# Gated stage of a fused fp32 kernel: order of the loads of x and the output's stores, half results from ScalarE's queue, order of the sums, and where the quarters of w3 · w_out are made

## The chip, the cores and the metric

The kernel runs on one core of one Trainium2 chip, as one launch. The time is the device time of the whole launch in microseconds (us).

## The reference

All tensors are float32. The kernel computes an attention with pooled keys and values, a mixture of four experts, and a gated layer, one after the other:

```python
k_p, v_p = k, v averaged over 8 neighbours          # batch 4, heads 8, seq 576, dim 64
attn = softmax(q @ k_p.T / 8) @ v_p                 # q: (4, 8, 576, 64)
x = attn, heads joined                              # (2304, 512)
p = domain_probs / sum(domain_probs)
x = sum over e of p[:, e] * (relu(x @ w1[e]) @ w2[e])    # 4 experts, 512 x 1024 and 1024 x 512
a = x @ w1                                          # moe2: (512, 1024)
b = x @ w2                                          # (512, 1024)
h = a * b @ w3                                      # a * b first; w3: (1024, 1024)
out = h @ w_out                                     # w_out: (1024, 512); out: (2304, 512)
```

## The kernel before

**Matmuls.** Each fp32 operand is split into a high part, rounded to the format that TensorE takes at full speed, and a low part, the difference. `hi_lo` does that: ScalarE copies the high part (L181), VectorE or GpSimd subtracts (L182). `mm3` (L176 to L178) makes one product of three matmuls: high by low, low by high, high by high. A 2 x 2 block product is done with seven block products instead of eight (Winograd's form of Strassen's method); the operands of these are the blocks A11, A12, A22 and the sums S1 to S4 of the left side, and B11, B21, B22 and T1 to T4 of the right side.

**The unit stage.** Since nothing stands between w3 and w_out, the kernel multiplies these two first: `w3_h` splits a piece of w3, and 24 units, run by `run_units` while the last expert ends (to 885.5 us), give the eight row blocks of w34 = w3 · w_out. `keep_w34` copies three (at last two) such blocks out of PSUM on ScalarE (L726) and stores them in DRAM (L727). Other work that belongs to the gated stage, the gate weights' sums and splits (`weights_of`, L797 to L800), stands between the units in a table `early`.

**The gated stage** (885.57 to 1270.5 us) goes over w34 in two halves, and in each half over the four batches of 576 tokens, in the order 2, 3, 0, 1. A batch has two parts. The first is four calls of `gated_rows(j)`; each makes a pair of row blocks of a and b with `seven` (products in the order p11, p22, p21, p12, and a `rest` of 18 matmuls, which `settle` runs inside the next call or inside the second part), multiplies them (L1390), sums and splits them into the right operand of the second part. The second part (84 matmuls) multiplies by a half of w34: p11 for the left column group, `settle`, p11 for the right one, p12, p22, p21, and then the sums (`add2`, L1501) by which the results are made out of the products. A batch has 252 matmuls in all.

In **half 0** the results are sums of half of the inner dimension: `give` copies them (L1481) and stores them in `half_d` through SyncE's queue (L1482), eight stores a batch. Beside it `prepare_x` makes the operand of x for the next batch (four subtractions L939 to L942, then splits), and `put_away` stores it in DRAM (`kept`) for half 1. In **half 1** `fetch_x` (L964) loads that operand back, in two pieces kc = 0 and kc = 1 of six transfers each; kc = 1 has about 2.0 MB. The halves are loaded (L1457); `give` adds (L1485), turns a tile of 128 x 288 on VectorE (L1487) into a buffer of `rawpool`, which has four such, and issues four stores of the output per tile (L1491), 32 a batch, all from SyncE's queue.

The pieces of w34 for a half (its A and S operands, `make_w34`, for n = 0 and 1) are made from rows loaded by `load_w34`, inside the first batch of each half, at j = 1 and 2. In the last batch of half 0 (called `swap` in the code) `weights_of` also makes the gate weights of half 1. PSUM banks come from a ring of eight; the first four products of a batch are written into the banks that p11[0], p11[1], p12[0] and p12[1] of the batch before had (the number in brackets is the column group g).

All instructions of an engine run in the order in which the code issues them. A transfer is issued by an engine's queue, also in order: where one has to wait, those behind it wait too.

## Time and profile before

| | before |
|---|---|
| median of 3 runs | 1274.4 us (1273.94 to 1275.97) |
| profiled execution | 1272.21 us, span of its profile 1270.5 us |
| busy: TensorE, VectorE, ScalarE, GpSimd | 1170.4 (92%), 767.1 (60%), 466.3 (37%), 514.8 us (41%) |
| mean granted clock of TensorE | 0.97 of full |

The span is the stretch that the profile covers; the execution's own time is 1.7 us longer. PE is TensorE's matmuls, PEld its weight loads, DVE VectorE, ACT ScalarE, POOL GpSimd, SP SyncE; SPq and ACTq are the queues in which SyncE and ScalarE issue transfers. PEclk is the clock granted to TensorE as a share of full speed. A time in square brackets is how long the engine stood idle before that instruction, with what ended the wait. Busy shares are means over the whole span, and the stages differ.

### The profile page before, as it was taken

The page shows a single profiled execution, that of the slowest core. Times are in us where ns is not written, and L with a number is a line of the kernel's source. Part 1 is how long each engine was busy: PE and PEld are TensorE (multiplying, and loading weights), DVE is VectorE, ACT ScalarE, POOL GpSimd, SP SyncE. Part 2 cuts the span into 40 slices and gives each one's busy share as a digit, 9 for nine tenths or more (in the row PEclk, how much of TensorE's full clock was granted, in tenths as well). Part 3 has the DMA queues.
Part 4 walks back from the last instruction along what each step waited for, and adds up shares of the span by engine and source line. Part 5 has one row for each costly group of instructions (what it writes and reads, how often), then busy time and mean ns, then how long its engine had stood idle before and what let it go on. Part 6 is the DMA issues. An engine that isn't in the chain of part 4 may idle for free.

```text
span 1270.5 us, 20381 instructions
## 1 busy us (share of the span) xinstructions
PE 1170.4 (92%) x7034; PEld 1065.5 (84%) x7034; DVE 767.1 (60%) x1615; ACT 466.3 (37%) x1029; POOL 514.8 (41%) x597
## 2 busy tenths in 40 slices
PE   8999999999999999999999999999799987595874
PEld 6888889998988988998998998888798887495774
DVE  6766534654666665666656677566666676544634
ACT  4543332453412542422552421545444444231221
POOL 6955113454525565525674534400512245220211
PEclk9999999999999999999999999999899998897978
DMA  8963623557767367658467868566554367345242
GB/s 212 225 157 78 209 94 137 203 185 241 252 212 221 108 213 218 216 151 263 121 191 218 237 152 242 141 167 178 202 205 160 138 206 241 83 123 143 77 126 38
DMA packets 278040, 221.81 MB, mean 175 GB/s; under 512 B 132528, under 2 KB 232880, under 8 KB 277936
## 3 DMA queue, kind: packets, MB, share of 16 engines
q1 hardware_dynamic: 277648, 219.98, 57.6%
q8 instruction: 55, 0.90, 0.3%
q10 hardware_dynamic: 288, 0.52, 0.1%
q14 instruction: 49, 0.40, 0.1%
HBM read 146.51 MB, written 73.92 MB: 174 GB/s over the span
## 4 chain that ended last, share of the span: by engine, by line
PE 75%; DVE 10%; DMA 5%; ACT 4%; issue 3%; SPq 2%; POOL 1%; DVEq 0%; ACTq 0%; POOLq 0%
PE g L177 13%; PE g L176 13%; PE g L178 13%; PE s L176 11%; PE s L178 10%; PE s L177 10%; PE sc L506 1%; PE x_ps L560 1%; DMA xo<-kept 1%; DVE plain L1381 1%; ACT round L181 1%; PE at_ps L545 1%; SPq L1491 1%; DVE plain L1390 1%; DVE x5l L1381 1%
## 5 line engine op out<-in xcount | busy, mean ns | idle before, releaser
L182 POOL TENSOR_TENSOR round<-plain,round 128x576 fp32r<-128x576 f32 (+1 forms) x130 | 178.5, 1376 | 403.9 <-ACT round L181 305.6
L176 PE MATMUL s<-xo,wh 128*128 128x288 f32 x840 | 255.2, 304 | 41.6 <-DMA xo<-kept 30.8
L178 PE MATMUL s<-xo,wh 128*128 128x288 f32 x840 | 252.3, 300 | 0.0
L177 PE MATMUL s<-xo,wl 128*128 128x288 f32 x840 | 251.5, 299 | 0.0
L176 PE MATMUL g<-w,round 128*128 128x512 f32 x540 | 211.7, 392 | 0.0
L177 PE MATMUL g<-w,round 128*128 128x512 f32 x540 | 211.2, 391 | 0.1
L178 PE MATMUL g<-w,round 128*128 128x512 f32 x540 | 210.9, 391 | 0.0
L176 PEld LDWEIGHTS s<-xo,wh 128*128 128x128 f32 x840 | 161.7, 193 | 47.4 <-DMA xo<-kept 32.6
L177 PEld LDWEIGHTS s<-xo,wl 128*128 128x128 f32 x840 | 162.1, 193 | 1.0
L178 PEld LDWEIGHTS s<-xo,wh 128*128 128x128 f32 x840 | 162.2, 193 | 0.0
L1004 ACT ACTIVATE plain<-s 128x288 f32<-128x288 f32 x80 | 32.7, 408 | 257.7 <-PE s L178 256.5
L1000 DVE TENSOR_TENSOR s<-s,plain 128x288 f32<-128x288 f32 x160 | 73.7, 461 | 78.3 <-PE s L178 75.2
L178 PEld LDWEIGHTS g<-w,round 128*128 128x128 f32 x540 | 101.3, 188 | 21.5
L176 PEld LDWEIGHTS g<-w,round 128*128 128x128 f32 x540 | 101.5, 188 | 20.1 <-issue 0.8
L177 PEld LDWEIGHTS g<-w,round 128*128 128x128 f32 x540 | 101.4, 188 | 19.6 <-DVE round L698 0.4
L181 ACT ACTIVATE round<-plain 128x576 fp32r<-128x576 f32 (+2 forms) x147 | 90.5, 626 | 45.7 <-DVE plain L1381 31.0
L294 POOL TENSOR_TENSOR x5l<-x5l 128x256 uint32<-128x256 uint32 x80 | 59.3, 741 | 117.3 <-DVE x5l L293 115.8
L1222 ACT ACTIVATE plain<-s 128x288 f32<-128x288 f32 x144 | 53.0, 403 | 95.0 <-PE s L178 88.7
L176 PE MATMUL s<-round,w 128*128 128x288 f32 x224 | 68.8, 307 | 19.5 <-DVE plain L1390 8.6
L1000 DVE TENSOR_TENSOR plain<-s,pb 128x288 f32<-128x288 f32 x72 | 32.9, 458 | 62.6 <-ACT pb L1010 34.6
L1000 DVE TENSOR_TENSOR plain<-s,plain 128x288 f32<-128x288 f32 x80 | 36.2, 453 | 53.1 <-PE s L178 46.4
L698 DVE SCALAR_TENSOR_TENSOR round<-g,round 128x384 fp32r<-128x384 f32 x48 | 26.6, 553 | 69.1 <-ACT round L697 68.8
(270 smaller groups left out, 2550.3 us busy)
## 6 DMA issues: line engine op xcount, KB each, us to landing
xo<-keptx SPq DMA_DIRECT2D x63, 576.0 KB
raw<-in_moe_w_dram SPq DMA_DIRECT2D x64, 256.0 KB
plain<-acc SPq DMA_DIRECT2D x40, 256.0 KB
keptx<-xo SPq DMA_DIRECT2D x16, 576.0 KB
x5h<-in_moe_w_dram SPq DMA_DIRECT2D x128, 64.0 KB
x5h<-in_moe_w_dram SPq DMA_DIRECT2D x32, 256.0 KB
kept<-xo SPq DMA_DIRECT2D x12, 576.0 KB
acc<-plain SPq DMA_DIRECT2D x26, 256.0 KB
```

Source lines behind the costliest of these rows:

```text
L176: nc.tensor.matmul(ps, lh, rl, start=first, stop=False, skip_group_check=onto)
L177: nc.tensor.matmul(ps, ll, rh, start=False, stop=False, skip_group_check=onto)
L178: nc.tensor.matmul(ps, lh, rh, start=False, stop=last, skip_group_check=onto)
L181: nc.scalar.activation(hi, src, AF.Copy)
L182: (lo_eng or nc.vector).tensor_tensor(lo, src, hi.bitcast(F32), op=ALU.subtract)
L294: nc.gpsimd.tensor_tensor(au, au, bu, op=ALU.add)
L506: nc.tensor.matmul(sc[off:off + n, (hp % 2) * W:(hp % 2 + 1) * W], qT[:, hp, off:off + n], kT_t[b][:, hp * W:(hp + 1) * W], start=True, st ...
L698: nc.vector.scalar_tensor_tensor(hl, ps, 0.0, hh.bitcast(F32), op0=ALU.max, op1=ALU.subtract)
L1000: nc.vector.tensor_tensor(to, one, two, op=ALU.add)
L1004: nc.scalar.activation(x, p11, AF.Copy)
L1222: nc.scalar.activation(c[:, a], c[:, a] if bank is None else bank, AF.Relu)
L1381: nc.vector.tensor_tensor(to, one, two, op=op)
```

## The change

It does five things, all in the gated stage and the unit stage.

1. **Loads of x.** In half 1, the fetch of kc = 1 is called right after `settle` in the second part, so its six transfers stand in SyncE's queue ahead of all 32 stores of the batch; before, they stood between the two groups of 16. In half 0 the same call makes the four subtractions of `prepare_x` at that place, the first splits come ahead of the results, and the loads of the batch after next are issued earlier (`load_x`).
2. **Half results.** In half 0, six of a batch's eight half stores are issued by ScalarE, behind the copy that makes them; two stay in SyncE's queue.
3. **The order of the sums.** Both products p11 now stand ahead of `settle`. VectorE makes the sums with p12 for both column groups, then those with v, and only then the results are given. In `gated_rows` for j >= 2 the second multiplication follows the first.
4. **Quarters of w34.** The pieces for half 0 are made between the units, in four steps each, at units 10, 11, 13, 14 and 18, 19, 21, 22, with both splits on ScalarE and VectorE. Three of the four rows that they need stay in SBUF; the row of block 1 is stored, and read back into the place that block 5 had. In half 1 the pieces stay at j = 1 and 2, with A11 and S1 split on VectorE instead of GpSimd.
5. **Turned tiles** go to a ring of five buffers (`turns`) instead of four.

The core of the diff:

```diff
         def keep_w34(b, pss):
             for o, ps in enumerate(pss):
-                t = kept_rows.tile([P, DM], F32)
-                nc.scalar.activation(t, ps, AF.Copy)
-                nc.sync.dma_start(w34_d[w3_blocks[b][0] + o], t)
...
+                fc = w3_blocks[b][0] + o
+                t = row_tile((0, 1, 2, 2, 1, 0, 3, 3)[fc])
+                nc.scalar.activation(flat2(t), ps, AF.Copy)
+                if fc in (0, 2, 3):
+                    w34_raw[fc] = t
+                else:
+                    nc.sync.dma_start(w34_d[fc], flat2(t))
+            if b == 1:
+                w34_raw[1] = row_tile(0)
+                nc.sync.dma_start(flat2(w34_raw[1]), w34_d[1])
...
+            def one():
+                left, right = w34_raw[n], w34_raw[n + 2]
+                w34_raw["s"] = s()
+                nc.vector.tensor_tensor(w34_raw["s"][:, 0], left[:, 1], right[:, 1], op=ALU.add)
+                nc.vector.tensor_tensor(w34_raw["s"][:, 1], w34_raw["s"][:, 0], left[:, 0], op=ALU.subtract)
+                split(A11, left[:, :1], nc.vector)
+
+            def two():
+                left = w34_raw[n]
+                nc.vector.tensor_tensor(left[:, 1], left[:, 0], left[:, 1], op=ALU.subtract)
+                split(S1, w34_raw["s"], nc.vector)
+
+            def three():
+                split(A12, w34_raw[n + 2], other)
+
+            def four():
+                left, right = w34_raw.pop(n), w34_raw.pop(n + 2)
+                nc.vector.tensor_tensor(left[:, 0], right[:, 0], w34_raw.pop("s")[:, 1], op=ALU.subtract)
+                split(S3, left[:, 1:], other)
+                split(S4, left[:, :1], other)
...
+        for n, at in enumerate((10, 18)):
+            for m in range(4):
+                early.setdefault(at + m + (m > 1), []).append(lambda n=n, m=m: w34_pieces(n, lambda: row_tile(1), nc.vector)[m]())
...
+        turns = row(x5[0], 0, HALF_ROW, 5)
...
-                        nc.sync.dma_start(half_d[b][:, m, a * HB:(a + 1) * HB], ob)
+                        (nc.sync if ps is None else nc.scalar).dma_start(half_d[b][:, m, a * HB:(a + 1) * HB], ob)
...
-                    tt = rawpool.tile([P, HB], F32, tag="raw", name="tt")
+                    tt = turns.tile([P, HB], F32)
...
-                p11 = [bank_s()]
-                second_part(p11[0], 0, A11, B11, two)
-                nc.scalar.activation(x[0], p11[0], AF.Copy)
+                p11 = []
+                for g in two:
+                    p11.append(bank_s())
+                    second_part(p11[g], g, A11, B11, two)
+                    nc.scalar.activation(x[g], p11[g], AF.Copy)
                 settle()
-                p11.append(bank_s())
-                second_part(p11[1], 1, A11, B11, two)
-                nc.scalar.activation(x[1], p11[1], AF.Copy)
+                ahead = half == 0 and n_b < B - 2
+                next_x(1, first, 0)
+                if ahead:
+                    load_x(g_order[n_b + 2], 0)
...
                 for g in two:
                     second_part(p11[g], g, A12, B21, [1])
-                    if half:
-                        add2(halves[:, g + 2, 1], halves[:, g + 2, 1], v[g])
-                        ob = halves[:, g + 2, 1]
-                    else:
-                        ob = place(g + 2, 1)
-                    add2(ob, p12[g], ob if half else v[g])
+                for g in two:
+                    add2(obs[g], p12[g], obs[g] if half else v[g])
                     add2(p12[g], p12[g], u[g])
+                next_x(1, first, 1)
+                if half:
+                    for g in two:
+                        add2(obs[g], obs[g], v[g])
+                for g in two:
                     give(g, 0, p11[g])
-                    give(g + 2, 1, None, ob)
-                next_x(1, first, 0)
+                    give(g + 2, 1, None, obs[g])
```

**SyncE's queue, end of half 1's first batch and start of its second.** Before (`out_dram` is the output, `half_...` the stored halves, `kept` the stored operand of x, and w_68, round and edge the places that it is loaded into):

```order
L1457 DMA plain<-half_8717 128x576 x4
L1491 DMA out_dram<-tt 32x9x32 x16
L964 DMA w_68<-kept 128x288
L964 DMA w_68<-kept 128x576
L964 DMA round<-kept 128x1152
L964 DMA edge<-kept 128x288
L964 DMA round<-kept 128x576
L964 DMA edge<-kept 128x1152
L1491 DMA out_dram<-tt 32x9x32 x16
```

And now:

```order
L1485 DMA plain<-half_8743 128x576 x4
L987 DMA w_68<-kept 128x288
L987 DMA w_68<-kept 128x576
L987 DMA round<-kept 128x1152
L987 DMA edge<-kept 128x288
L987 DMA round<-kept 128x576
L987 DMA edge<-kept 128x1152
L1519 DMA out_dram<-x5h 32x9x32 x32
```

The six transfers out of `kept` have moved ahead of the first 16 stores, and the two groups of 16 stand together.

**VectorE, second part of the last batch.** Before, from the fifth sum on (s_12059 and s_12060 are the banks of p12, s_12075 and s_12076 those of p21; plain holds the halves, tt the turned tiles):

```order
L1501 TENSOR_TENSOR plain<-plain,pb 128x288
L1501 TENSOR_TENSOR plain<-s_12059,plain 128x288
L1501 TENSOR_TENSOR s_12059<-s_12059,plain 128x288
L1485 TENSOR_TENSOR plain<-s_12009,plain 128x288
L1487 STREAM_TRANSPOSE tt<-plain 128x288 x2
L1501 TENSOR_TENSOR plain<-plain,pb 128x288
L1501 TENSOR_TENSOR plain<-s_12060,plain 128x288
L1501 TENSOR_TENSOR s_12060<-s_12060,pb 128x288
L1485 TENSOR_TENSOR plain<-s_12051,plain 128x288
L1487 STREAM_TRANSPOSE tt<-plain 128x288 x2
L1485 TENSOR_TENSOR plain<-s_12075,plain 128x288
L1487 STREAM_TRANSPOSE tt<-plain 128x288
```

And now, from the last of ten sums on (here s_12023 and s_12024 are the banks of p12, s_12039 and s_12040 those of p21, and x5h holds the turned tiles):

```order
L1529 TENSOR_TENSOR plain<-plain,pb 128x288 x2
L1513 TENSOR_TENSOR plain<-s_11973,plain 128x288
L1515 STREAM_TRANSPOSE x5h<-plain 128x288 x2
L1513 TENSOR_TENSOR plain<-s_11981,plain 128x288
L1515 STREAM_TRANSPOSE x5h<-plain 128x288 x2
L1513 TENSOR_TENSOR plain<-s_12039,plain 128x288
L1515 STREAM_TRANSPOSE x5h<-plain 128x288
L1513 TENSOR_TENSOR plain<-s_12040,plain 128x288
L1515 STREAM_TRANSPOSE x5h<-plain 128x288
L1513 TENSOR_TENSOR plain<-s_12023,plain 128x288
L1515 STREAM_TRANSPOSE x5h<-plain 128x288
L1513 TENSOR_TENSOR plain<-s_12024,plain 128x288
```

Eight additions stood ahead of the first transpose, and eleven do now; the additions that read p12's banks stand ahead of the seventh and of the eighth transpose, as before.

**VectorE, near the end of the unit stage.** Before (raw holds a piece of w3, edge and round its low halves; wl are low halves of gate weights):

```order
L182 TENSOR_TENSOR wl<-plain,wh 128x512
L182 TENSOR_TENSOR wl<-plain,wh 128x256
L182 TENSOR_TENSOR round<-raw,round 128x256
L182 TENSOR_TENSOR edge<-raw,edge 128x256
L182 TENSOR_TENSOR wl<-x5l,wh 128x768
L182 TENSOR_TENSOR round<-x5l,round 128x256
L182 TENSOR_TENSOR edge<-raw,edge 128x256
L182 TENSOR_TENSOR round<-raw,round 128x256
```

And now (plain holds the rows of w34, w_68 the pieces' low halves):

```order
L756 TENSOR_TENSOR plain<-plain 128x256
L757 TENSOR_TENSOR plain<-plain 128x256
L182 TENSOR_TENSOR w_68<-plain,w_68 128x256
L182 TENSOR_TENSOR round<-raw,round 128x256
L762 TENSOR_TENSOR plain<-plain 128x256
L182 TENSOR_TENSOR w_68<-plain,w_68 128x512
L182 TENSOR_TENSOR edge<-raw,edge 128x256
L182 TENSOR_TENSOR wl<-x5l,wh 128x768
L182 TENSOR_TENSOR round<-x5l,round 128x256
L182 TENSOR_TENSOR edge<-raw,edge 128x256
L182 TENSOR_TENSOR w_68<-plain,w_68 128x512
L182 TENSOR_TENSOR round<-raw,round 128x256
```

The second piece's steps stand among the low halves of the units; L756 is the first operation that reads the row of block 1.

## Rows read from the trace of the kernel before

**Rows 1.** The chain that ended last, by engine (page)

```profile
PE 75%; DVE 10%; DMA 5%; ACT 4%; issue 3%; SPq 2%; POOL 1%; DVEq 0%; ACTq 0%; POOLq 0%
```

**Rows 2.** Windows: stretch length, busy by engine (instructions), granted clock, DMA share, GB/s

```profile
885.57:932.07 46.50, 39.01 (x255) 37.91 (x254) 29.69 (x61) 19.93 (x48) 20.73 (x20) 0.89 0.46 162
...
932.07:1048.45 116.38, 104.74 (x755) 100.70 (x754) 78.70 (x168) 52.19 (x122) 32.01 (x32) 1.00 0.53 189
...
1048.45:1098.90 50.45, 38.31 (x255) 36.05 (x254) 33.78 (x71) 20.99 (x52) 27.48 (x26) 0.93 0.46 152
...
1098.90:1254.65 155.75, 112.93 (x759) 107.87 (x757) 72.88 (x176) 34.50 (x84) 28.19 (x30) 0.85 0.41 113
```

**Rows 3.** Windows, two stretches of half 1's last batch

```profile
1217.64:1220.52 2.88, 2.88 (x13) 2.88 (x13) 0.92 (x2) 0.16 (x1) 0.00 (x0) 0.50 0.40 66
...
1226.00:1238.03 12.03, 11.91 (x90) 11.67 (x88) 6.41 (x16) 3.82 (x10) 3.44 (x4) 1.00 0.12 44
```

**Rows 4.** Waits, batches 1 to 3 of half 1: total, times, longest

```profile
PE s L176 <- DMA xo<-kept: 24.8, 4, 11.9
...
PE s L176 <- DMA edge<-kept: 11.8, 2, 11.5
...
PE s L176 <- DVE s L1501: 3.4, 3, 1.1
```

**Rows 5.** Timeline of SyncE's queue: start, length, what, count

```profile
1200.29 7.80 SPq L1491 DMA_DIRECT2D out_dram<-tt  x16
...
1208.19 2.77 SPq L964 DMA_DIRECT2D xo<-kept  x6
...
1211.06 10.46 SPq L1491 DMA_DIRECT2D out_dram<-tt  x16
```

**Rows 6.** Timeline of TensorE: start, length, what [idle before]

```profile
1213.88 0.61 PE L176 MATMUL s<-xo,wh 128*128 128x288 f32 x1 [10.54 <-DMA xo<-kept]
...
1217.24 0.61 PE L176 MATMUL s<-xo,wh 128*128 128x288 f32 x1 [1.55 <-DMA xo<-kept]
```

**Rows 7.** Timeline of VectorE in the last batch

```profile
1248.10 0.46 DVE L1501 TENSOR_TENSOR plain<-s,plain 128x288 f32<-128x288 f32 x1 [2.26 <-PE s L178]
...
1251.65 0.84 DVE L1487 STREAM_TRANSPOSE tt<-plain 128x288 f32<-128x288 f32 x2
...
1257.41 0.48 DVE L1487 STREAM_TRANSPOSE tt<-plain 128x288 f32<-128x288 f32 x1 [1.27 <-DMA out_dram<-tt]
```

**Rows 8.** Timeline of SyncE's queue, last batch

```profile
1252.15 15.98 SPq L1491 DMA_DIRECT2D out_dram<-tt  x32
```

**Rows 9.** Timeline of TensorE, half 1, batch 0, 25th matmul

```profile
1061.05 0.29 PE L176 MATMUL s<-xo,wh 128*128 128x288 f32 x1
```

**Rows 10.** Timeline of ScalarE, from half 0 to half 1

```profile
1053.72 0.69 ACT L1481 ACTIVATE plain<-s 128x288 f32<-128x288 f32 x2
```

**Rows 11.** Waits, first batch of half 0

```profile
PE s L176 <- DVE plain L1390: 7.2, 3, 3.6
```

**Rows 12.** Timeline of VectorE, last units and first gated batch

```profile
876.78 0.42 DVE L799 TENSOR_TENSOR x5l<-plain 128x256 f32<-128x256 f32 x1
...
877.45 1.02 DVE L182 TENSOR_TENSOR wl<-plain,wh 128x512 fp32r<-128x512 f32 x2
...
892.93 0.46 DVE L939 TENSOR_TENSOR x5h<-plain 128x288 f32<-128x288 f32 x1 [2.98 <-DMA plain<-turned]
```

**Rows 13.** Timeline of TensorE, unit stage

```profile
872.55 0.50 PE L177 MATMUL g<-round,edge 128*128 128x512 f32 x1 [0.58 <-DVE edge L182]
```

**Rows 14.** Timeline of ScalarE, unit stage

```profile
873.32 1.99 ACT L726 ACTIVATE plain<-g 128x512 f32<-128x512 f32 x3 [0.71 <-PE g L178]
```

**Rows 15.** Timeline of TensorE, second part of a batch of half 0

```profile
954.74 0.37 PE L176 MATMUL s<-round,w 128*128 128x288 f32 x1 [0.48 <-DVE plain L1390]
...
963.35 0.40 PE L176 MATMUL s<-round,w 128*128 128x288 f32 x1 [0.38 <-ACT pb L1509]
```

**Rows 16.** Timeline of ScalarE's queue, first loads of the kernel

```profile
0.81 0.88 ACTq L405 DMA_DIRECT2D plain<-in_k_dram  x2
```

More of the change, by code (lines that the diff above doesn't have):

```diff
@@ L719, in fused_kernel, with row_tile, flat2 @@
         w34_t.update((n, tuple(Ring(w2_area, [(2 * n + m) * W34]).tile([P, 7, 2 * P], F32R) for m in range(2))) for n in range(2))
-        kept_rows = row(plain, 0, ROW, 3)
+        stage_rows = [Ring(plain, [ROW * n]) for n in range(4)]
         w34_raw = {}
+        def row_tile(n):
+            return stage_rows[n].tile([P, 2, 2 * P], F32)
+        def flat2(t):
+            return t.rearrange("p a m -> p (a m)")
         def keep_w34(b, pss):
             for o, ps in enumerate(pss):
-                t = kept_rows.tile([P, DM], F32)
-                nc.scalar.activation(t, ps, AF.Copy)
-                nc.sync.dma_start(w34_d[w3_blocks[b][0] + o], t)
@@ new lines, in keep_w34, with load_w34 @@
+                t = row_tile((0, 1, 2, 2, 1, 0, 3, 3)[fc])
[7 more added lines that the diff above has]
+                nc.sync.dma_start(flat2(w34_raw[1]), w34_d[1])
+        def load_w34(n):
+            for fc in (n, n + 2):
+                w34_raw[fc] = rawpool.tile([P, 2, 2 * P], F32, tag="raw", name="w34r")
+                nc.sync.dma_start(flat2(w34_raw[fc]), w34_d[NJ + fc])
@@ new lines, in w34_pieces, with split @@
+        def w34_pieces(n, s, other):
+            def split(a, src, eng):
+                m = src.shape[1]
+                hi_lo(*(flat2(t[:, a:a + m]) for t in w34_t[n]), flat2(src), eng)
+            def one():
[15 more added lines that the diff above has]
+                split(S4, left[:, :1], other)
+            return one, two, three, four
@@ L1402, in sink @@
                     mult(1)
+                    mult(0)
                     add(up[:, 1], g[:, 1], up[:, 1])
@@ L1406, in sink @@
                         split_g(n, T2, up[:, :1], VE)
-                    mult(0)
-                    if n:
                         split_g(n, T3, up[:, 1:], VE)
@@ L1443, in fused_kernel @@
                         weights_of(3)
-                    if n_b == 0 and j in (1, 2):
-                        make_w34(j - 1)
-                    if n_b == 0 and j < 2:
-                        load_w34(half, j)
+                    if half == 1 and n_b == 0 and j in (1, 2):
+                        for f in w34_pieces(j - 1, lambda: rawpool.tile([P, 2, 2 * P], F32, tag="raw", name="w34s"), nc.gpsimd):
+                            f()
+                    if half == 1 and n_b == 0 and j < 2:
+                        load_w34(j)
                     if half == 0 and n_b == 0 and j < 2:
@@ L1523, in fused_kernel @@
                     add2(u[g], p22[g], x[g])
+                obs = [place(g + 2, 1) for g in two]
                 for g in two:
@@ L1544, in fused_kernel @@
                     give(g + 2, 0, p21[g])
-                next_x(1, first, 1)
                 next_x(1, first, 2)
+                if ahead:
+                    load_x(g_order[n_b + 2], 1)
                 if swap:
@@ L1551, in fused_kernel @@
                     give(g, 1, p12[g])
-                if half == 0 and n_b < B - 2:
-                    for kc in range(2):
-                        load_x(g_order[n_b + 2], kc)
                 put_away()
```

19 lines of the change are left out of this document (removed).

## The prediction

> **What bounds the kernel now.** I read the chain that ended last first: three quarters of the span run over TensorE [rows 1], so a change pays only where TensorE stands still or runs slowly. Then I cut the gated stage into stretches that end where a batch's last matmul ends [rows 2]. A batch always has 252 matmuls. At the full granted clock one takes 12.03/90 = 0.1337 us, in a low stretch 2.88/12 = 0.24 us (12 of the 13 start in it) [rows 3], so a batch needs 252 x 0.1337 = 33.7 us. Half 0 (its last three batches: 116.38, or 38.8 each) is near that; half 1 is not: 155.75 for batches 1 to 3, or 51.9 each, at clock 0.85. The waits of that stretch [rows 4] say why: TensorE stood 24.8 + 11.8 = 36.6 us for transfers out of kept. In SyncE's queue [rows 5] those six transfers start only when the first 16 stores of the output have been issued (1200.29 to 1208.09), and TensorE, which ran dry at 1203.3, gets its two pieces at 1213.88 and 1217.24 [rows 6]; the second is 9.05 us after the first issue. Behind each such wait comes a stretch at clock 0.50.
>
> **1. The fetch ahead of the stores (half 1, batches 1 to 3).** The six transfers are now issued when the second part's first products are set going, 84 - 12 = 72 matmuls or 9.6 us before the boundary T (I write T for the end of a batch's last matmul). By the 5.7 to 9.05 us of [rows 5, 6] the data lie there between T - 4 and T - 0.5; they are needed at T + 0.4 at the earliest. So the waits for kept go, and the low clock with them.
>
> What is late next is VectorE. In the last batch [rows 7] the first sum starts at u0 = 1248.10, the first transpose at u0 + 3.55, and the first store [rows 8] at s0 = u0 + 4.05; 32 stores take 15.98, so 2.0 per tile. The sixth transpose waits 1.27 for a buffer and starts at s0 + 5.26: with four buffers the k-th starts at s0 + 2.0 (k - 4) + 1.25. After, eleven additions stand ahead of the first transpose instead of eight. Eight took 3.55, 0.44 each with their small waits; three more, back to back at some 0.3 to 0.4, make s0 = u0 + 5.0, less if the small waits go: I take u0 + 4.9. That is about T - 0.1, as TensorE has some 38 of the 84 matmuls left at u0 (5.0 us). With five buffers the sixth transpose starts at s0 + 3.25, the seventh at s0 + 5.25. The additions that read the last two banks (those of p12) stand behind these two on VectorE, and the next batch's third and fourth products write into these banks. The first is free at about T + 3.15 + 0.48 + 0.46 = T + 4.1, with the semaphore T + 4.15; TensorE wants it 12 matmuls after T, at T + 1.6: **2.55 us of wait**. The second is free at T + 6.15 and wanted at T + 4.95: **1.2 us more**. The 3.4 us in three waits for the sums [rows 4] go, since the sums now stand ahead of the transposes. New length of a batch: 33.7 + 3.75 = 37.45. Gain: 155.75 - 3 x 37.45 = **43.4 us**. Bounds: without any boundary wait 54.6; with twice it 32; if such a wait again drops the clock, as the wait of 10.54 did for some 20 matmuls (six of the first piece, and 3.3/0.24 = 14 from 1217.24 to 1220.52, [rows 3, 6]), 20 x 0.106 = 2.1 per batch less.
>
> **2. The last batch's end.** Nothing runs beside the last 32 stores. They start 0.85 later after u0 (4.9 instead of 4.05), while TensorE's 1.1 us stall before them goes; the span then ends s0 + 18.35 as now (1252.15 to 1270.50). Measured from the end of the batch, which part 1 counts, the stores begin at T - 0.1 instead of T - 2.5: **-2.4 us** (0 to -2.5).
>
> **3. Half 1, batch 0.** Before, its 25th matmul started at 1061.05 [rows 9], after the same two waits for kept and with its first matmuls at 0.24. After, the fetch precedes the gate loads and the half stores, and the third product waits for what now comes last: ScalarE's copies of the p12 banks at 1053.72 [rows 10], which stand behind the last of the new weights' splits; that work is not moved. First copy done 1054.1, 25th matmul at about 1054.6: **+6.4 us**. Bounds: 3, if the splits get later by the sums moved in front of them; 9, if they get earlier with the second part.
>
> **4. Quarters of w3 · w_out made between units.** The first gated batch loses its stalls for VectorE's L1390, which stood behind the pieces: 7.2 us in three [rows 11], and its low clock (0.89 of 46.50, [rows 2]). It should come near its neighbours' 38.8, with less to wait for at its start: 36 to 38, so +8.5 to +10.5; I take 10. The work goes into the unit stage. Of the two pieces' 18 VectorE operations, 14 are 128x256 at about 0.42 and 4 are 128x512 at 0.51 [rows 12]: 14 x 0.42 + 4 x 0.51 = 7.9 us. TensorE already waited there once for a low half (0.58, [rows 13]), and the low halves stand behind the pieces in VectorE's order; I charge 1.5 for that. The second piece needs the row that is read back: ScalarE's copies end at 875.3 [rows 14], the store has to be issued (0.5) and land (1.25, the buffer waits of [rows 7]), and the row has to come back, nearly 3 us as the reload that VectorE waited 2.98 for [rows 12]; so 880 to 881, where the unit's slot is at 877. The low half behind it is 4 late: 1.5 + 4 = 5.5. A clock that falls after such a wait costs 2.1 as above; I charge 1.5. Net 10 - 5.5 - 1.5 = **+3 us**. Bounds: -4 (all 7.9 on TensorE, 4 of wait, 2.1 of clock) and +7 (1.5 and 1.5 only).
>
> **5. Half 0's second part, three batches.** The product before settle takes away the two waits of 0.48 and 0.38 where TensorE stood for L1390 and for a copy [rows 15], with the slower first matmul behind each some +1.4 a batch. Against it, four subtractions (4 x 0.46 = 1.8) stand ahead of the sums, of which I let 0.75 reach TensorE, and six half stores are issued by ScalarE; an issue took 0.88/2 = 0.44 there [rows 16], so four of them put the next operand's last split off by 1.8, of which I let 1.05 through, as VectorE waits for ScalarE there only part of the time: 1.4 - 0.75 - 1.05 = -0.4 a batch. Over three batches **-1 us** (-4 to +3).
>
> The Trainium skill, "DMA: Bandwidth & Descriptors", section "Issuing engines are not separate DMA queues", says that transfers issued from several engines share the same 16 DMA engines and that only the issuing sequencer's time is saved, usually little. By it the move to ScalarE's queue saves SyncE about 6 issues a batch and nothing else. [Rows 16] agree as far as they go (a like issue time), and this is one reason why I give the move no gain; the sum is the same with or without the rule.
>
> **Sum.** 43.4 - 2.4 + 6.4 + 3 - 1 = 49.4. The profiled execution took 1272.2 (span 1270.5), so 1222.8; the median of the runs, 1274.4, is 2.2 higher, which gives **1225 us**.
>
> **Rivals.**
> A. The boundary wait doesn't come about, because VectorE runs through the reordered sums faster than I count: 49.4 + 3 x 3.75 = 60.7, so 1214; with part 4 at its best 1210. Against it: four stores per tile at 2.0 us are slower than VectorE's 0.94 per tile (0.46 + 0.48, [rows 7]), so some buffer must be waited for. Chance 0.12; range 1206 to 1214.
> B. Parts 3 to 5 go to their low bounds: the unit stage pays in full, ScalarE's issues stand in the splits' way. 43.4 - 2.4 + 3 - 4 - 4 = 36, with the clock falling at boundaries (3 x 2.1) 30: 1238 to 1244, and to 1255 if the boundary wait is twice as long too. For it: VectorE is nearly full in the unit stage. Chance 0.16.
> C. The fetch still comes late: it waits for its target's last reader, or its 2.0 MB and the halves' loads share the DMA engines. Then 36.6 us of wait shrink by no more than the 7.8 of the 16 stores: 3 x 8 = 24, less 2.4 and the rest at zero: 1250 to 1272. Against it: the target is the operand that this batch's rows have finished with by settle. Chance 0.06.
> D. Slower: TensorE's clock. A stretch at 0.50 costs 252 x (0.24 - 0.1337) = 26.8 us a batch. If the new, shorter but more frequent waits keep the granted clock low for more than 49.4/0.106 = 466 matmuls, not quite two batches, beyond today's, the gain is eaten, and it ends at 1277 or more. Against it: after a wait of 10.54 the clock stood at 0.50 until 1220.5 and at 1.00 from 1226 on [rows 3, 6]. Chance 0.04.
>
> **How the numbers follow.** The forecast, with 2 to 5 us left at each boundary, has 0.62 and its own range is 1214 to 1237. The 80% range reaches into A and B: 1208 to 1244. A, B, C and most of the forecast's tails are faster by more than 0.2% (2.5 us, about what a measurement tells from no change): 0.95; same 0.01; slower 0.04.
>
> **What would show it.** In the profile after: no wait of TensorE for kept in half 1 over 1 us; batches there of 36 to 39 us at clock 1.0; waits of TensorE for the additions of the last two banks, 2 to 3 and 1 us, and VectorE's transposes waiting for stores; a first gated batch of 36 to 38; the unit stage ending at about 891 instead of 885.6; the third product of half 1 waiting for ScalarE. I am wrong if batches 1 to 3 still hold waits for kept, or if the clock in half 1 stays under 0.95.

## The result and the profile after

| | before | changed |
|---|---|---|
| median | 1275.18 us (1273.94 to 1275.99, 4 runs) | 1235.78 us (1233.16 to 1236.57, 4 runs) |
| ratio | | 0.9688 (95% interval 0.9671 to 0.9706) |
| span of the profiled execution | 1270.5 us | 1231.4 us |

The changed kernel is 39.4 us faster; 49.4 had been forecast (to 1225 us), with a range of 1208 to 1244. The windows by stretch answer to [rows 2], this time cut where a batch's first matmul starts; the first is the first batch of half 0, then come three batches, the first batch of half 1, three batches, and the kernel's end:

```profile
895.42:934.09 38.67, 34.82 (x254) 33.71 (x252) 25.60 (x55) 15.75 (x38) 9.75 (x10) 1.00 0.51 180
934.09:1053.00 118.91, 105.68 (x759) 103.85 (x757) 78.91 (x167) 54.06 (x124) 34.25 (x33) 0.97 0.56 199
1053.00:1095.60 42.60, 36.44 (x255) 35.13 (x254) 31.96 (x72) 20.05 (x49) 22.21 (x22) 0.96 0.52 176
1095.60:1213.76 118.16, 109.92 (x758) 107.44 (x756) 71.00 (x175) 34.13 (x84) 28.93 (x30) 0.93 0.47 131
1213.76:1231.40 17.64, 0.16 (x2) 0.00 (x0) 4.43 (x11) 0.00 (x0) 0.00 (x0) 0.56 0.40 67
```

I took each batch's length from the start of its first matmul to that of the next batch's first:

| stretch | before | changed | difference |
|---|---|---|---|
| start of the gated stage | 885.57 | 895.42 | +9.85 |
| half 0, first batch | 46.23 | 38.67 | -7.56 |
| half 0, three more | 37.80 + 37.79 + 41.19 | 40.30 + 37.19 + 41.42 | +2.13 |
| half 1, first batch | 50.44 | 42.60 | -7.84 |
| half 1, three more | 50.67 + 53.09 + 51.87 | 39.56 + 38.94 + 39.66 | -37.47 |
| behind the last matmul | 15.85 | 17.64 | +1.79 |

The sum is -39.1, the difference of the spans. Of the 9.85 at the start, 1.8 were there before the units: the last 174 matmuls ahead of the gated stage begin at 846.83 instead of 845.07. They take 48.6 us instead of 40.5, so 8.1 arise in the unit stage. In four other runs with the same unit stage (below) they take 47.4 to 47.9, and the gated stage begins at 892.5 to 893.7.

In SyncE's queue of the changed kernel the fetch of kc = 1 now stands ahead of 32 stores in one row (the answer to [rows 5]; its last transfer is shown):

```profile
1087.48 0.43 SPq L987 DMA_DIRECT2D edge<-kept  x1
1095.23 16.96 SPq L1519 DMA_DIRECT2D out_dram<-x5h  x32
```

The last of six issues for kc = 1 is over at 1087.9, 7.7 us ahead of the boundary at 1095.60. No wait of TensorE for kept is left in half 1. What it waits for instead, in the timeline of TensorE at that boundary (the answer to [rows 6]):

```profile
1099.31 0.40 PE L176 MATMUL s<-xo,wh 128*128 128x288 f32 x1 [1.97 <-DVE plain L1513]
...
1101.22 0.61 PE L176 MATMUL s<-xo,wh 128*128 128x288 f32 x1 [0.65 <-DVE plain L1513]
1101.62 0.44 PE L177 MATMUL s<-xo,wl 128*128 128x288 f32 x1
1101.86 0.44 PE L178 MATMUL s<-xo,wh 128*128 128x288 f32 x1
```

The 13th matmul of the batch waits 1.97 and the 19th 0.65 for VectorE's L1513, the addition in `give`, and from there on the matmuls follow each other at 0.24 us, the step of the low clock. VectorE at the same place (the answer to [rows 7]):

```profile
1090.48 0.46 DVE L1529 TENSOR_TENSOR plain<-s,plain 128x288 f32<-128x288 f32 x1 [0.92 <-PE s L178]
...
1094.72 0.84 DVE L1515 STREAM_TRANSPOSE x5h<-plain 128x288 f32<-128x288 f32 x2
...
1098.43 0.48 DVE L1515 STREAM_TRANSPOSE x5h<-plain 128x288 f32<-128x288 f32 x1 [0.46 <-DMA out_dram<-x5h]
1098.83 0.42 DVE L1513 TENSOR_TENSOR plain<-s,plain 128x288 f32<-128x288 f32 x1
1100.34 0.48 DVE L1515 STREAM_TRANSPOSE x5h<-plain 128x288 f32<-128x288 f32 x1 [1.09 <-DMA out_dram<-x5h]
1100.74 0.42 DVE L1513 TENSOR_TENSOR plain<-s,plain 128x288 f32<-128x288 f32 x1
1102.41 0.48 DVE L1515 STREAM_TRANSPOSE x5h<-plain 128x288 f32<-128x288 f32 x1 [1.25 <-DMA out_dram<-x5h]
```

The sixth, seventh and eighth transposes wait 0.46, 1.09 and 1.25 for stores, and each of the additions at 1098.83 and 1100.74, which free the two banks, stands behind one of them. The sixth starts 3.20 behind the first store's issue, the seventh 5.11, the eighth 7.18; 3.25, 5.25 and 7.25 had been worked out.

### The profile page after: what moved, and what is told of

It is laid out like the page before. It is cut to its first block, busy times and chain, and to the rows that moved or that the text cites. A ratio compares the mean times of both kernels' runs of the same rounds, so it can differ in the third digit from the quotient of the medians.

```text
span 1231.4 us, 20352 instructions
## 1 busy us (share of the span) xinstructions
PE 1167.4 (95%) x7034; PEld 1065.5 (87%) x7034; DVE 767.7 (62%) x1629; ACT 466.6 (38%) x1029; POOL 502.0 (41%) x583
## 4 chain that ended last, share of the span: by engine, by line
PE 77%; DVE 8%; DMA 5%; SPq 3%; issue 3%; ACT 3%; POOL 1%; ACTq 0%; DVEq 0%; POOLq 0%
PE g L177 12%; PE g L178 12%; PE g L176 12%; PE s L176 12%; PE s L178 12%; PE s L177 12%; PE sc L506 1%; DMA x5h<-in_moe_w_out_dram 1%; PE x_ps L560 1%; PE at_ps L545 1%; SPq L1519 1%; DMA out_dram<-x5h 1%; SPq L475 1%; DVE plain L1529 1%; ACT round L181 1%
## 5 line engine op out<-in xcount | busy, mean ns | idle before, releaser
L182 POOL TENSOR_TENSOR round<-plain,round 128x576 fp32r<-128x576 f32 (+1 forms) x130 | 178.2, 1374 | 389.1 <-ACT round L181 175.7
L176 PEld LDWEIGHTS s<-xo,wh 128*128 128x128 f32 x840 | 159.9, 190 | 20.2 <-DVE plain L1513 6.7
L178 PEld LDWEIGHTS s<-xo,wh 128*128 128x128 f32 x840 | 160.0, 191 | 0.0
L1023 DVE TENSOR_TENSOR s<-s,plain 128x288 f32<-128x288 f32 x160 | 73.8, 461 | 73.9 <-PE s L178 70.1
L181 ACT ACTIVATE round<-plain 128x576 fp32r<-128x576 f32 (+2 forms) x147 | 90.5, 626 | 47.4 <-DVE plain L1408 33.8
L176 PE MATMUL s<-round,w 128*128 128x288 f32 x224 | 68.2, 305 | 10.6 <-ACT pb L1559 9.4
L1023 DVE TENSOR_TENSOR plain<-s,pb 128x288 f32<-128x288 f32 x72 | 33.0, 458 | 61.8 <-ACT pb L1033 35.5
L178 PE MATMUL s<-round,w 128*128 128x288 f32 x224 | 67.4, 301 | 0.0
```

Source lines behind the costliest of these rows:

```text
L176: nc.tensor.matmul(ps, lh, rl, start=first, stop=False, skip_group_check=onto)
L178: nc.tensor.matmul(ps, lh, rh, start=False, stop=last, skip_group_check=onto)
L181: nc.scalar.activation(hi, src, AF.Copy)
L182: (lo_eng or nc.vector).tensor_tensor(lo, src, hi.bitcast(F32), op=ALU.subtract)
L1023: nc.vector.tensor_tensor(to, one, two, op=ALU.add)
```

## The experiments

Each time stands beside that of the kernel before on the same chip (medians 1274.3 in the first two groups of runs, 1277.0 in the last).

### Eight places for the turned tiles

```diff
-                    tt = turns.tile([P, HB], F32)
+                    k = turned_n[0] % 8
+                    turned_n[0] += 1
+                    tt = turns.tile([P, HB], F32) if k < 5 else rawpool.tile([P, HB], F32, tag="raw", name="tt")
```

> The changed kernel, with the turned tiles of half 1 in eight places instead of five (the last three of a batch in the pool of raw tiles), so that no transpose waits for stores within a batch; order and stores are the same. Theory (the 2.0 and 1.0 us that TensorE waits at the three boundaries of half 1 come from the transposes' waits, and the stretch at 0.24 us a matmul behind them comes from these waits): both go, batches 1 to 3 fall from 118.2 us together to 102 to 104, and the kernel takes 1219 to 1223 where the changed one takes 1235.8. Rival 1 (the low clock there has a cause of its own): the waits go and the slow matmuls stay, 1226 to 1228. Rival 2 (the banks are late because VectorE itself is late): no change, 1234 to 1237.

Measured: 1220.24 us, ratio 0.9575 (0.9555 to 0.9595). Windows of half 1's batches 1 to 3, first of the changed kernel:

```profile
1095.60:1135.16 39.56, 36.94 (x254) 36.09 (x253) 23.65 (x59) 11.37 (x28) 9.69 (x10) 0.91 0.57 165
1135.16:1174.10 38.94, 35.95 (x255) 35.23 (x254) 23.68 (x59) 11.38 (x28) 9.70 (x10) 0.96 0.57 168
1174.10:1213.76 39.66, 37.04 (x254) 36.12 (x252) 23.67 (x59) 11.38 (x28) 9.54 (x10) 0.91 0.27 61
```

and of the kernel with eight places:

```profile
1092.90:1128.46 35.56, 34.02 (x254) 33.49 (x253) 23.66 (x59) 11.37 (x28) 9.69 (x10) 1.00 0.63 183
1128.46:1164.23 35.77, 34.25 (x255) 33.73 (x254) 23.68 (x59) 11.39 (x28) 9.71 (x10) 1.00 0.62 183
1164.23:1200.40 36.17, 34.40 (x254) 33.58 (x252) 23.79 (x59) 11.46 (x28) 9.53 (x10) 1.00 0.30 67
```

The clock goes from 0.91, 0.96 and 0.91 to 1.00 and the batches to 35.6 to 36.2. The 19th matmul's wait is gone; the 13th still waits 1.5 (4.6 in three waits), as the additions stand behind five or six transposes even when these don't wait:

```profile
PE s L176 <- DVE plain L1514: 4.6, 3, 1.5
```

So the theory holds in part. The second wait and half a microsecond of the first came from the transposes' waits for stores; the rest of the first is VectorE's plain order, and the batches are 107.5 together, not 102 to 104. The slow matmuls are gone too. That they came from these waits is not shown by this alone: with all half stores on SyncE (below) the waits stay and the slow matmuls are gone all the same. Of the 13.4 us between the two profiled spans, 10.7 lie in these three batches; 2.9 were gained ahead of the gated stage, where the code is the same.

### The additions first, with five places

```diff
+                if half:
+                    late_turns = []
                 for g in two:
                     second_part(p21[g], g, A22, T4, two)
                     give(g + 2, 0, p21[g])
...
+                for args in late_turns or ():
+                    turn(*args)
```

From there on `give` only adds and notes the tile in `late_turns`; `turn` holds the transpose and the stores that stood in `give`.

> The changed kernel, with five buffers as it has, and in half 1 the four additions that read the banks of p21 and p12 ahead of the four last transposes of a batch, so that no bank waits behind a transpose that waits for stores. Theory (the banks' additions behind waiting transposes cost TensorE 2.0 and 0.8 us, and the clock fell by these): as with eight buffers, where 1.5 us and no low stretch were left, or better: VectorE adds as soon as a product is done, so no wait over 0.5 us is left; batches 1 to 3 take 34.0 to 34.6, together 102 to 104 instead of 118, and the kernel 1219 to 1223. Rival (the stores must drain anyway, so the wait comes back one batch later or at the end): batches of 35.5 or more, or a tail over 19 us; 1224 or more.

Measured: 1233.77 us, 0.9675 (0.9652 to 0.9698): no faster than the changed kernel. The rival was right. TensorE in the second batch of half 1:

```profile
1094.79 0.40 PE L176 MATMUL s<-xo,wh 128*128 128x288 f32 x1 [0.56 <-DVE plain L1513]
...
1102.02 0.40 PE L176 MATMUL s<-xo,wh 128*128 128x288 f32 x1 [3.00 <-ACT pb L1033]
```

The wait at the 13th matmul falls to 0.56, and one of 3.00 appears at the 43rd, for ScalarE's L1033. That copies v out of a sum which VectorE can only make when the last transposes, still waiting for stores, are behind it:

```profile
1098.45 0.48 DVE L1521 STREAM_TRANSPOSE x5h<-plain 128x288 f32<-128x288 f32 x1 [2.61 <-DMA out_dram<-x5h]
1100.07 0.48 DVE L1521 STREAM_TRANSPOSE x5h<-plain 128x288 f32<-128x288 f32 x1 [1.14 <-DMA out_dram<-x5h]
1100.47 0.42 DVE L1023 TENSOR_TENSOR plain<-s,plain 128x288 f32<-128x288 f32 x1
```

The waits of 2.61 and 1.14 for stores now stand behind the additions that free the banks, but ahead of the next batch's sums (L1023). The three batches take 37.98, 39.92 and 40.65.

### The fetch alone, in the kernel before

```diff
                 settle()
+                if half:
+                    next_x(1, first, 0)
...
-                next_x(1, first, 0)
+                if not half:
+                    next_x(1, first, 0)
```

> The kernel before, with one edit: in half 1 the fetch of kc = 1 is called right after settle. Theory (nearly the whole gain is the fetch ahead of the stores, and what takes its place is VectorE's wait for buffers): no wait for kept over 1 us in batches 1 to 3; with four buffers and s0 at T - 2.5 the sixth transpose starts at about T + 2.75, so TensorE waits 2 us and then 1 us as in the changed kernel and still 1.1 us for the sums; these batches take 39.5 to 41 each, 155.6 becomes 119 to 123, and the kernel takes 1238 to 1243. Rival (the fetch comes late all the same without the reordered sums, or the other edits carry half of the gain): over 1250.

Measured: 1245.44 us, 0.9771 (0.9746 to 0.9796). The waits of TensorE in half 1's batches 1 to 3, to be laid beside [rows 4]:

```profile
PE s L176 <- DVE plain L1485: 9.4, 6, 2.0
...
PE s L176 <- DVE s L1501: 3.4, 3, 1.1
```

No wait for kept is left; 9.4 us of waits for the additions take the place of 36.6, and the 3.4 for the sums stay. These batches take 40.09 + 43.38 + 41.55 = 125.0 instead of 155.6. So this one edit brings 29 of the 39 us. It came out 2 us over the expected range; behind the waits in two of the three batches stand 16 and 11 slow matmuls (27 x 0.106 = 2.9 us). The remaining 10 us are shared out by the stretches of the profile alone: no run has the other edits without this one.

### The row of block 1 kept in SBUF

```diff
-                t = row_tile((0, 1, 2, 2, 1, 0, 3, 3)[fc])
+                t = row_tile((0, 1, 2, 2, 3, 0, 0, 3)[fc])
...
-            if b == 1:
-                w34_raw[1] = row_tile(0)
-                nc.sync.dma_start(flat2(w34_raw[1]), w34_d[1])
```

The sums go to place 3. In the first of two runs they overwrite a tile of the expert stage that is still wanted, so that part of its output is wrong, and its time is not that of a whole kernel; in the second run the first piece starts three units later, and all is computed.

> The changed kernel, with the row of block 1 kept in SBUF instead of stored and read back (another order of the four places: block 4 goes to place 3, block 5 and 6 to place 0, the sums to place 3). Theory (of the 9.85 us by which the unit stage ends later, the read back costs 2.85 us of wait, about 0.9 behind it and some 2.5 at the low clock): the unit stage ends 5 to 6 us earlier, 1229 to 1232. Rival (the pieces' own work on VectorE and ScalarE is the cost, and TensorE waits for low halves wherever they stand): less than 2 us, 1234 to 1237.

> As the run before with the row of block 1 kept in SBUF, and with the first piece's four steps at units 13, 14, 15 and 16 instead of 10, 11, 13 and 14, by when the place of its sums is free. In the other run the unit stage ended 7.8 us earlier than in the changed kernel, and the first gated batch took 36.3 instead of 38.7. Theory (the read back was the cost, in both): the same here within 1.5 us, 1223 to 1227. Rival (the low halves of the units are now behind both pieces in the last third, and TensorE waits there again): the unit stage ends only 3 to 5 us earlier, 1228 to 1232.

Measured: 1224.07 us, 0.96 (0.9579 to 0.962), and 1226.63 us, 0.9607 (0.9577 to 0.9637). TensorE's waits in the changed kernel's unit stage:

```profile
868.60 0.50 PE L177 MATMUL g<-round,edge 128*128 128x512 f32 x1 [0.98 <-DVE edge L182]
...
875.54 0.49 PE L176 MATMUL g<-round,edge 128*128 128x512 f32 x1 [0.53 <-ACT edge L181]
...
885.16 0.80 PE L176 MATMUL g<-round 128*128 128x512 f32 x1 [2.85 <-ACT round L181]
```

The last one is for a high half that ScalarE makes behind A11's split, which waits for the row that comes back; VectorE waited for that row too:

```profile
884.46 0.42 DVE L756 TENSOR_TENSOR plain<-plain 128x256 f32<-128x256 f32 x1 [2.42 <-DMA plain<-w]
```

Without the read back the gated stage begins at 887.59 and at 891.15, instead of 895.42 (892.5 to 893.7 in the other runs). The last 174 matmuls ahead of it take 41.9 and 44.0, where those with the read back take 47.4 to 48.6 and the kernel before 40.5. In the second run one wait of 2.20 for a low half (VectorE's L182) is left near the end of the unit stage, and the first gated batch takes 38.79. So the read back was the largest cost, as the theory has it: 3.5 to 4.6 of the 6.9 to 8.1 us go with it. By its time (1226.63) the second run lies where the theory had it, by the end of its unit stage (4.3 us earlier) where the rival had it, and for the rest the rival holds: with both pieces in the last third, the low halves come late again.

### The pieces back in the first gated batch

```diff
-        for n, at in enumerate((10, 18)):
-            for m in range(4):
-                early.setdefault(at + m + (m > 1), []).append(lambda n=n, m=m: w34_pieces(n, lambda: row_tile(1), nc.vector)[m]())
...
-                    if half == 1 and n_b == 0 and j in (1, 2):
+                    if n_b == 0 and j in (1, 2):
```

> The changed kernel, with the pieces of w34 for half 0 made again in the first gated batch, from rows that are stored and loaded (A11 and S1 split on VectorE, the rest on GpSimd). Theory (moving them gained 7.6 us in the first batch and cost some 8 in the unit stage): the unit stage ends some 8 us earlier, the first batch takes 45 to 47 instead of 38.7, and the time is that of the changed kernel within 2 us, 1234 to 1238. Rival (the move gained what was forecast, 3 us): 1239 or more. Rival 2 (it lost): 1232 or less.

Measured: 1233.34 us, 0.9684 (0.9658 to 0.971), which is the changed kernel's ratio. The gated stage begins at 884.45, and the first batch takes 49.22 with a clock of 0.90, more than the 45 to 47 expected:

```profile
884.45:933.67 49.22, 39.13 (x253) 38.23 (x252) 33.12 (x67) 20.85 (x50) 15.37 (x16) 0.90 0.50 172
```

What the move gained in the first batch it lost in the unit stage; it is worth nothing as it stands.

### The subtractions behind the sums

```diff
                 settle()
-                next_x(1, first, 0)
-                if ahead:
-                    load_x(g_order[n_b + 2], 0)
+                if half:
+                    next_x(1, first, 0)
...
                     add2(p12[g], p12[g], u[g])
+                if not half:
+                    next_x(1, first, 0)
+                if ahead:
+                    load_x(g_order[n_b + 2], 0)
                 next_x(1, first, 1)
```

> The changed kernel, with the four subtractions of prepare_x in half 0 behind the sums with p12 and u instead of ahead of all sums; half 1 is the same. Theory (the 2.1 us that TensorE waits for ScalarE's copy of v in each batch of half 0 is these subtractions, which take 3.3 us together while GpSimd works, ahead of the sums): this wait goes in batches 0, 1 and 2 of half 0; the wait at the boundary (1.0 to 2.7 us) stays or grows by up to 1, since the operand's splits stand behind the subtractions: 4 to 6 us less, 1230 to 1232. Rival (the boundary takes back what the sums gain): no change within 1.5 us.

Measured: 1229.94 us, 0.9647 (0.9627 to 0.9667). The waits of TensorE in half 0's first three batches, in the changed kernel:

```profile
PE s L176 <- ACT pb L1559: 6.5, 3, 2.3
...
PE s L176 <- DVE xo L182: 2.4, 1, 2.4
...
PE s L176 <- DVE edge L182: 1.0, 1, 1.0
```

and in the run with the subtractions behind the sums:

```profile
PE s L176 <- DVE edge L182: 2.6, 1, 2.6
PE s L176 <- DVE xo L182: 2.5, 1, 2.5
```

The 6.5 us for the copy of v are gone, the boundaries' waits go from 3.4 to 5.1, and the three batches from 116.2 to 112.3. The theory holds for half 0, with the part that the boundary takes back.

The edit does one thing more than its expectation says. In the last batch of half 0 the call that moves is not the subtractions but the fetch of kc = 1 for half 1. It is issued 5.8 us ahead of half 1's first batch (14.5 in the changed kernel), and that batch takes 45.03 instead of 42.60, with waits for kept again:

```profile
PE s L176 <- DMA xo<-kept: 3.4, 2, 2.5
```

### All half stores on SyncE

```diff
-                        (nc.sync if ps is None else nc.scalar).dma_start(half_d[b][:, m, a * HB:(a + 1) * HB], ob)
+                        nc.sync.dma_start(half_d[b][:, m, a * HB:(a + 1) * HB], ob)
```

> The changed kernel, with all half stores of half 0 issued by SyncE again. Theory (each issue costs ScalarE 0.45 us between copies, so the next operand's last split starts 1.3 to 1.8 later than it could and TensorE waits 1.0 to 2.7 us at the boundaries of half 0): these three waits shrink by about 1 each, and with them a low stretch of 1.9 us at two of them: 3 to 6 us less, 1230 to 1233. Rival 1 (the half stores then hold up the stores of the operand in SyncE's queue, and the splits wait for these): no change or up to 3 us slower. Rival 2 (the copies wait for TensorE anyway): no change.

Measured: 1227.93 us (1223.4 to 1232.13), 0.9642 (0.9614 to 0.9669). The gain is not where the theory had it: half 0 takes 156.5 instead of 157.6, and the boundaries' waits 4.8 in three instead of 6.1. Half 1, whose code is the same, gives the rest: its batches 1 to 3 take 37.16, 37.43 and 37.23, together 6.3 us less than in the changed kernel. Two of these windows:

```profile
1091.73:1128.89 37.16, 34.33 (x254) 33.54 (x253) 23.69 (x59) 11.35 (x28) 9.72 (x10) 1.00 0.61 176
1128.89:1166.32 37.43, 34.50 (x255) 33.75 (x253) 23.68 (x59) 11.36 (x28) 9.71 (x10) 1.00 0.61 175
```

And TensorE's timeline at the start of the first of them:

```profile
1095.45 0.40 PE L176 MATMUL s<-xo,wh 128*128 128x288 f32 x1 [1.97 <-DVE plain L1513]
...
1097.37 0.40 PE L176 MATMUL s<-xo,wh 128*128 128x288 f32 x1 [0.86 <-DVE plain L1513]
```

The clock stays at 1.00 after waits of 1.97 and 0.86, behind which it fell to 0.5 in the changed kernel (1.97 and 0.65). So what the edit brings by its own queue is about 2 us: 1.1 in half 0, and 1.0 in half 1's first batch, whose 13th matmul waits 1.12 instead of 2.38 for ScalarE's copy. Most of the gain in this profile hangs on where the clock fell; why it didn't here is open. The profiled execution is the fastest of four (1223.4, with a mean clock of 0.987); the slowest took 1232.13 at 0.978, about as long as the changed kernel's fastest (1233.16 at 0.977).

### Five edits together, and two queues at the end

The eight places, the additions first, the row kept (with the first piece at units 13 to 16), the subtractions behind the sums and the half stores on SyncE; and then in the last batch

```diff
-                        nc.sync.dma_start(to.rearrange("(b i) j -> i b j", i=32),
+                        (nc.scalar if last and q % 2 else nc.sync).dma_start(to.rearrange("(b i) j -> i b j", i=32),
```

> The changed kernel with five edits together: eight places for turned tiles, the additions of p21 and p12 ahead of the last four transposes, the row of block 1 kept in SBUF, the subtractions behind the sums, all half stores on SyncE. Theory (each edit takes away a wait of its own): half 1's batches 1 to 3 at 34.0 to 34.8 with no wait over 0.6 us, since no addition stands behind a transpose that waits (with five buffers the additions' wait came back 30 matmuls later at ScalarE's copy); the unit stage ends 4 us earlier; half 0's batches 0 to 2 at 35 to 37, with 1 to 2 us at the boundary: 1205 to 1213. Rival (the operand's last split at the boundaries of half 0 grows by what the earlier sums gain, and the low stretches stay): 1214 to 1220.

> As the run with five edits, and in the last batch every second store of the output issued by ScalarE, which has no other work then. Theory (the end of the kernel is 32 issues of 0.5 us in one queue): the last stores take 8 to 9 us instead of 16, VectorE's additions and transposes (0.94 a tile) become the next bound, and the kernel is 6 to 8 us faster than that one. Rival (the transfers and not the issues take the time, so that two queues share one rate): less than 2 us faster.

Measured: 1207.86 us, 0.9464 (0.9435 to 0.9493), and 1198.64 us, 0.9387 (0.9355 to 0.942). Half 1's batches 1 to 3 take 34.5 to 34.7 each, with one wait of 0.52 to 0.56 left in each. At each of half 0's three boundaries 2.1 us of wait are left, where 1 to 2 were expected. The end of the run with one queue, in SyncE's queue:

```profile
1185.35 9.80 SPq L1525 DMA_DIRECT2D out_dram<-x5h  x20
1195.25 5.88 SPq L1525 DMA_DIRECT2D out_dram<-tt  x12
```

With two, SyncE's queue:

```profile
1187.40 4.95 SPq L1525 DMA_DIRECT2D out_dram<-x5h  x10
1192.45 3.01 SPq L1525 DMA_DIRECT2D out_dram<-tt  x6
```

and ScalarE's:

```profile
1187.41 5.02 ACTq L1525 DMA_DIRECT2D out_dram<-x5h  x10
1192.53 3.01 ACTq L1525 DMA_DIRECT2D out_dram<-tt  x6
```

32 issues of 0.49 in one queue (15.8 us) become 16 in each of two (8.1), and the stretch behind the last matmul goes from 17.9 to 10.2. The medians differ by 9.2 us, a little more than expected. The rival (one shared rate of transfer) is out at this size of transfer. Both versions are faster than the kernel before and the changed one. Both hold the moved fetch too: in half 1's first batch TensorE waits for kept, 1.39 and 1.54 with one queue, 1.57 and 1.71 with two.

## Why the prediction was right, and where it was off

**Part 1 (43.4 forecast, 37.5 measured).** The mechanism came as described, at every step: the fetch early enough, the sixth transpose at s0 + 3.2, two waits, 2.1 and 1.0 us by the gap between the matmuls' starts (2.26 and 1.10 at the first boundary, less 0.13) where 2.55 and 1.2 had been worked out. The term was mis-sized by one sentence, which stood among its bounds: "if such a wait again drops the clock ... 2.1 per batch less". It did in all three batches of the profiled execution: 22, 12 and 22 matmuls ran at 0.24 us, 56 x 0.106 = 5.9 us, as much as this term was too large. (The waits were some 0.6 a batch shorter than worked out, and small delays elsewhere made up for that.) That the clock falls after so short a wait was in no row of before, where it fell after waits of 2.65 to 11.9 and stayed up after others of 3.0 and 3.2; it belonged into the forecast with a chance and not into the bounds. By the prediction's own sign, a clock in half 1 under 0.95, this point was wrong: the clock was 0.96 in the first batch and 0.93 in the other three. The batches of 38.9 to 39.7 came at 0.91 to 0.96 and not at 1.0.

**Part 2 (-2.4 forecast, -1.8 measured).** Right; the end is bound by issues, as the run with two queues shows.

**Part 3 (+6.4 forecast, +7.8 measured).** The wait is the one that was named: the 13th matmul of half 1, which begins the third product, waits for ScalarE's copy of p12 (L1509) and no longer for kept.

```profile
1057.13 0.40 PE L176 MATMUL s<-edge,wh 128*128 128x288 f32 x1 [2.38 <-ACT plain L1509]
```

That the number is near is in part luck. With a first copy done at 1054.1 the third product would start there, and the 25th matmul 12 matmuls later, at 1055.7 and not at 1054.6; and the matmul of [rows 9] is the batch's 28th, as three run ahead of the wait for kept. So its own figures give some 5. The copy was done earlier than worked out (the 13th matmul starts 4.1 us behind the batch's start, where 5.5 follow from 1054.1), and up to the 28th matmul the batch gained 6.2. Its second part gained 2.4 more, as waits of 0.41, 0.26 and 1.12 are gone there that the sum did not hold, and what lies between lost 0.8. No run tests this part by itself.

**Part 4 (+3 forecast, -2.3 measured).** The place of the cost was right (the row read back, 2.85 us of TensorE's wait after 4 had been estimated), and so, nearly, was its size: 5.5 + 1.5 = 7 had been charged for the unit stage, and it was 8.1 in the profiled execution and 6.9 to 7.4 in four others. The step that failed is the gain of the first batch, 7.6 and not 10: it has the 2.26 us of wait of part 5, which I had charged to three batches only. The remaining 1.8 us at the start of the stage came from before the units, where nothing was changed. With the pieces put back the time is the same within the interval, so the move gains nothing.

**Part 5 (-1 forecast, -2.1 measured).** The waits of [rows 15] went, as forecast. The four subtractions cost more than 0.75: TensorE waits 2.1 us for the copy of v behind them in the second and third batch (2.26 in the first), and behind two of the waits in these three batches stand 14 slow matmuls each, 28 x 0.106 = 3.0 us that the term did not hold. VectorE's timeline at that place in the second batch of the changed kernel:

```profile
964.51 1.06 DVE L962 TENSOR_TENSOR x5h<-plain 128x288 f32<-128x288 f32 x1
965.60 0.95 DVE L963 TENSOR_TENSOR x5h<-plain,x5h 128x288 f32<-128x288 f32 x1
966.47 1.06 DVE L964 TENSOR_TENSOR x5h<-plain 128x288 f32<-128x288 f32 x1
967.45 0.45 DVE L965 TENSOR_TENSOR x5h<-plain,x5h 128x288 f32<-128x288 f32 x1
```

And GpSimd's timeline there:

```profile
964.16 3.06 POOL L182 TENSOR_TENSOR round<-x5l,round 128x288 fp32r<-128x288 f32 x3 [2.67 <-ACT round L181]
```

The three that run while GpSimd splits (964.16 to 967.22) take 1.06, 0.95 and 1.06; the fourth, behind it, 0.45, and all four took 0.45 or 0.46 with the subtractions behind the sums, where GpSimd had ended. The sum of 4 x 0.46 held rows of VectorE alone, and 3.5 us was the price at that place. This agrees with the Trainium skill, "SBUF — State Buffer", section "Who interferes with whom": a VectorE instruction with both inputs in SBUF contends with a GpSimd instruction that reads SBUF. I had not asked which engine works beside a moved instruction.

**The rivals.** A (no boundary wait) is what eight places and the additions first give, but not this kernel. Of B came the clock that falls at the boundaries, 5.9 of the missing 10.3 us; the unit stage cost 8.1, nearer to the 7 charged than to B's 14. The other misses are the first batch (2.4), the unit stage (1.1), the 1.8 from before it and part 5 (1.1), less 2.0 that parts 2 and 3 brought beyond their terms. C and D did not come about: no wait for kept is left in half 1, and its clock rose from 0.93 and 0.85 in [rows 2] to 0.96 and 0.93.

The Trainium skill's rule in the prediction ("DMA: Bandwidth & Descriptors", "Issuing engines are not separate DMA queues") also says that the sequencer's time saved by a second issuing engine is usually small. At the end of this kernel it is 7.7 us of 17.9, and the measurement decides: with 36 KB per issue of 0.49 us the issuing queue was the bound.

## What to carry to other kernels

When a large wait is taken away, work out the next one in line on the same engine, and then ask what the clock does behind it: here more than half of the missing gain went into matmuls at half speed after waits of some 2 us. An instruction in an ordered queue that waits for a buffer delays all behind it; putting others ahead of it only moves the wait to the next that stand behind, so it is the buffers that have to be added, and then the order pays too: batches 1 to 3 of half 1 take 118.2 us in the changed kernel, 118.6 with the other order, 107.5 with more buffers, and 103.9 in the run that has both among its five edits. A moved instruction costs what it costs at its new place, beside the engines that work there; and a call that does one thing in most batches and another in the last moves both.

## What the runs showed of the hardware that was not expected

- After waits of about 2 us TensorE's clock fell to 0.5 of full in some places and not in others with the same waits: in the changed kernel 22, 12 and 22 matmuls in a row at 0.24 us behind the three boundaries of half 1, and none with the half stores on SyncE, after 1.97 and 0.86. In half 0 the wait of 2.11 at the same matmul was followed by such a stretch in the second batch and not in the third. With the fetch alone, waits of 1.80 and 1.03 at one boundary of half 1 left the clock up, and 1.79 and 1.03 two batches later brought it down. What decides it is open.
- A single store of 36 KB costs the issuing queue 0.49 us, and two queues issue at twice the rate (32 in 8.1 us).
